# The second MLP's 36 token tiles as nodes of the list scheduler, with TensorE products costed shorter than they are

## The chip, the cores and the metric

The kernel runs on one core of a Trainium2 chip. The metric is the device time of one execution in microseconds (us). Before the change it is 1145.37 us, the median of three runs (1145.16 to 1147.82).

## What is computed

The inputs are float32, the two MLPs' weights float64. An attention with a packed middle step feeds a first MLP (512 to 2048 to 512, ELU), and that feeds the second MLP, which is what the change touches. The reference, cut to that part:

```python
x = _moe_ref(x=attention(q, k, v, p), ...)          # 4608 tokens x 512
def _moe2_ref(x, w_in, w_out, g_ln):
    h = x @ w_in                                     # 4608 x 1024
    e = np.exp(h - np.max(h, axis=-1, keepdims=True))
    solu = h * e / (np.sum(e, axis=-1, keepdims=True) + 1e-09)
    mu = np.mean(solu, axis=-1, keepdims=True)
    var = np.mean((solu - mu) ** 2, axis=-1, keepdims=True)
    ln = (solu - mu) / np.sqrt(var + 1e-06) * g_ln
    return (ln @ w_out).astype(np.float32)           # 4608 x 512
```

## The kernel before, in words

Every matmul operand is split into a rounded high part and a low remainder, and a product is three matmuls (`mm3`, L62 to L66). The split is a copy to the high part on ACT (L152) and a subtraction on DVE (L154).

**First part.** Attention and first MLP are written as nodes. A node (L591) has an engine, a planned duration, what it needs, which buffers it takes and frees, and a due time. `order()` (L889) is a list scheduler with a clock of its own: it works out for each node the latest start that still meets the due times (`late`), and then goes forward, always placing the node that can start first, and among those of one engine that can start within 0.3 us the one with the smallest `late`. Each engine runs its nodes in the order in which they were placed. This is fixed for PE, DVE, ACT and SP by `tc.manual_schedule` (L1015). The first MLP is 256 steps; a step is `ffn_h` (6 matmuls), two ACT passes (L433, L434), a DVE pass (L439), the split (L446, L449) and `ffn_x2` (12 matmuls). Its result is stored to DRAM (`x_dram`).

**Second MLP.** 4608 tokens are 36 tiles of 128. Nine loads (`load_x2`, L497) bring four tiles each, into the slots `wo0` to `wo2` or `wo3` to `wo5` in turn. Per tile i:

- `split_x2` (L504): one ACT cast and one DVE subtraction;
- `h2_mm` (L509): 24 matmuls of 128x512 into a two-bank PSUM tile: the single `misc` tile or one of two `acc` tiles, by i;
- `solu_ln` (L520): DVE max (nm, L523), ACT exp (L526), DVE sum and reciprocal (L527, L529), DVE product (z, L532), ACT square (L535, which frees the PSUM tile), DVE scale (L536), POOL power (L538), DVE normalisation (ln, L540);
- `t2_blocks` (L543): a transpose in 32x32 blocks on DVE (L547) and 16 block moves, 8 on DVE (L555) and 8 on ACT (L557);
- `t2_a` (L560): the split of the transposed tile into slot `wo6` or `wo7` (lnT, L152 and L154);
- `out_mm` (L566): 24 matmuls of 128x512 (the last tile's in two halves of 256 columns), the copy from PSUM (y, L578, ACT) and the store (L579, SP).

Only the first load, the splits of tiles 0 and 1 and the first product are nodes (L872 to L877). The rest follows in the program from L1024 on. For PE that order is kept (L1023): h2(0) among the last first-MLP steps, h2(1), h2(2), then h2(3), out(0), h2(4), out(1), ..., h2(35), out(32), out(33), out(34), out(35). For DVE, ACT and SP the framework orders these instructions itself with a timeline of its own, and can place them among the nodes of the first part:

```python
    for i in range(NTT):
        if i + 3 < NTT:
            h2_mm(i + 3)
        if i + 1 < NTT:
            t2_a(i + 1)
        if i + 2 < NTT:
            t2_blocks(i + 2)
        if i + 3 < NTT:
            solu_ln(i + 3)
```

Of the kernel before, what the change touches and what calls it, by code (L numbers as in the profile page):

```python
# [34 lines left out]
def attention_mlp_kernel(ctx: ExitStack, tc: tile.TileContext, q, k, v, v_tail, p,  # L35
# [461 lines left out]
    def load_x2(t):  # L497
        raw = slot(f"x2raw{t}", [P, 4, BLK], f"wo{3 * (t % 2)}", F32)
        sp.dma_start(out=raw, in_=x2_dram[:, :, t * BLK:(t + 1) * BLK])
        hi = slot(f"x2hi{t}", [P, 4, BLK], f"wo{3 * (t % 2) + 1}", F32R)  # L500
        lo = slot(f"x2lo{t}", [P, 4, BLK], f"wo{3 * (t % 2) + 2}", F32R)
        xs[t] = raw, hi, lo
# [14 lines left out]
                    kk == 0, kk == 3)  # L517
        last["h2", i] = o

    def solu_ln(i):  # L520
        o = last.pop(("h2", i)).rearrange("p a c -> p (a c)")
        nm = small.tile([P, 1], F32, tag="nm", name=f"nm2_{i}")
        dve.tensor_reduce(out=nm, in_=o, axis=AX.X, op=ALU.max, negate=True)  # L523
        e = work.tile([P, 5 * 4 * D], F32, tag="k", name=f"e3_{i}", bufs=1)[:, 0:DFF2]
        sm = small.tile([P, 1], F32, tag="sm", name=f"sm2_{i}")
        act.activation(e, o, AF.Exp, bias=nm, accum_out=sm)  # L526
        dve.tensor_scalar(out=sm, in0=sm, scalar1=1e-9, scalar2=None, op0=ALU.add)  # L527
        r = small.tile([P, 1], F32, tag="r", name=f"r2_{i}")
# [12 lines left out]
        last["ln", i] = ln

    def t2_blocks(i):  # L543


        t = big.tile([P, 4 * HS], F32, tag="AT", name=f"lnB{i}", bufs=3)[:, 0:DFF2]
        dve.transpose(t, last.pop(("ln", i)))  # L547
        o = big.tile([P, 4 * HS], F32, tag="AT", name=f"lnX{i}", bufs=3)[:, 0:DFF2]
        tv = t.rearrange("p (c a n) -> p c a n", a=4, n=NP)
        ov = o.rearrange("p (c n) -> p c n", n=P)  # L550
        for r in range(4):
            for a in range(4):
                x, y = ov[a * NP:(a + 1) * NP, :, r * NP:(r + 1) * NP], tv[r * NP:(r + 1) * NP, :, a]
                if (r + a) % 4 < 2:
                    dve.tensor_copy(x, y)  # L555
                else:
                    act.copy(x, y)  # L557
        last["t2", i] = o

    def t2_a(i):  # L560
        o = last.pop(("t2", i))
        t = slot(f"lnT{i}", [P, 2, 8, P], f"wo{6 + i % 2}", F32R)
        both(split(t[:, 0].rearrange("p c n -> p (c n)"), t[:, 1].rearrange("p c n -> p (c n)"), o))
        last["lnT", i] = t

    def out_mm(i):  # L566
        t = last.pop(("lnT", i))
        n = DM if i < NTT - 1 else DM // 2
        for c in range(0, DM, n):
            o = h_ps(f"o{i}_{c}")[:, 0:n]  # L570
            for x in range(2):
                for kk in range(8):
                    w, cs = wo2[kk // 2], slice((kk % 2) * DM + c, (kk % 2) * DM + c + n)
                    pe.matmul(o, t[:, x, kk], w[:, 0, cs], start=x + kk == 0, stop=x == 1 and kk == 7)  # L574
                    if x == 0:
                        pe.matmul(o, t[:, 0, kk], w[:, 1, cs], start=False, stop=False)  # L576
            y = work.tile([P, DM], F32, tag="at", name=f"y{i}_{c}", bufs=3)[:, 0:n]
            act.copy(y, o)  # L578
            sp.dma_start(out=out[i * P:(i + 1) * P, c:c + n], in_=y)  # L579
# [7 lines left out]
    def node(name, eng, us, needs, emit, takes=(), lets=(), due=None, size=0, behind=()):  # L591
# [277 lines left out]
    for i in range(2):  # L869
        pass  # L870
    end_due = FIRST_US + STEP_US * len(steps)
    node(("x2raw",), SP, 0.4, [("xout", 0, 1, 15, i) for i in range(2)] + [("xout", 0, 0, 15, i) for i in range(2)],  # L872
         lambda: load_x2(0), takes=[("wo0", "x2raw"), ("wo1", "x2hi"), ("wo2", "x2lo")], size=1.0)
    for i in range(2):
        split_nodes(("x2", i), lambda i=i: split_x2(i), needs=[("x2raw",)])
    node(("h2", 0), PE, 5.6, [("spD", "x2", 0)] + [("wi2", j) for j in range(4)],
         lambda: h2_mm(0), takes=[("misc", "h2")], due=end_due + 2)  # L877
# [11 lines left out]
    def order():  # L889
# [13 lines left out]
        def latest(name):  # L903

            stack = [name]
            while stack:
                x = stack[-1]
                wait = [y for y in then.get(x, ()) if y not in late]
                if wait:
                    stack += wait  # L910
                    continue
                stack.pop()
                v = nodes[x]
                ends = [late[y] for y in then.get(x, ())]
                if v["due"] is not None:
                    ends.append(v["due"])
                late[x] = min(ends, default=1e9) - v["us"] - (LATENCY[v["eng"]] + v["size"] * 2.9
                                                              if v["eng"] == SP else max(0.06, LATENCY[v["eng"]]))
            return late[name]
        for x in nodes:  # L920
# [94 lines left out]
    with tc.manual_schedule(engines={getattr(mybir.EngineType, e) for e in ("PE", "DVE", "Activation", "SP")}):  # L1015
        for x in order():
# [10 lines left out]
    solu_ln(1)  # L1027
    both(split_x2(3))
    t2_blocks(0)
    t2_a(0)  # L1030
    load_x2(1)
    h2_mm(2)
    t2_blocks(1)
    solu_ln(2)
    for i in range(NTT):
        if i + 3 < NTT:
            h2_mm(i + 3)
        if i + 1 < NTT:
# [45 lines left out]
```

## Time and profile before

| | |
|---|---|
| median of three runs | 1145.37 us |
| the profiled execution, own time | 1142.79 us |
| its span, first to last instruction | 1141.0 us |
| PE busy | 1114.4 us (98%) |
| DVE / ACT / POOL busy | 868.5 / 750.7 / 20.4 us |
| second MLP, first product to end | 731.5 to 1141.0 us |
| mean granted TensorE clock | 0.994 |

Times in the rows are microseconds from the span's start unless marked ns. "L574 PE" is an instruction of line 574 on TensorE; `lnT<-lnX` is output and input by the program's tile names; x8 is a count of merged instructions. In brackets stands how long the engine sat idle before the instruction and who ended that. A matmul's end is modelled, so starts are the safer reading on PE. In the trace the h2 products appear as `h<-wi,x2hi` and the out products as `o<-wo,lnT`.

### The profile page before, as it was taken

To read this page: it belongs to the slowest core of one execution; us is meant where nothing else is said; L and a number is where in the kernel's file an instruction comes from. 1 tells how busy PE (TensorE), PEld (TensorE's weight loads), DVE (VectorE), ACT (ScalarE), POOL (GpSimd) and SP (SyncE) were. 2 spreads that over 40 slices of the span, in tenths; PEclk is the share of its full clock that TensorE was granted. 3 is DMA by queue.
4 is the path that set the end of the run, shared out by engine and by line. 5 is a ranking of instruction groups with operands and counts; after the bars stand their busy time and mean duration, and the time that the engine had idled before them with its cause. 6 is when DMAs were issued, how large, how long until landed. Compare 5 with 4: busy or idle time off the path is not lost.

```text
span 1141.0 us, 21041 instructions
## 1 busy us (share of the span) xinstructions
PE 1114.4 (98%) x8164; PEld 984.1 (86%) x8164; DVE 868.5 (76%) x1956; ACT 750.7 (66%) x1627; POOL 20.4 (2%) x42
## 2 busy tenths in 40 slices
PE   8799999999999999999999999999999999999997
PEld 7588898899899899899899899878888888888886
DVE  5899897678777778777778644588877878878775
ACT  4688865666666765666665555567776776676674
POOL 0000000000000000000000000000000000000000
PEclk9899999999999999999999999999999999999999
DMA  9957334024133124233122322610202101000001
GB/s 344 342 174 260 105 104 125 24 82 139 59 121 121 59 103 139 77 103 121 59 101 99 111 95 65 215 52 34 65 19 65 56 28 65 19 28 20 28 28 38
DMA packets 56116, 111.07 MB, mean 97 GB/s; under 512 B 4432, under 2 KB 32336, under 8 KB 54224
## 3 DMA queue, kind: packets, MB, share of 16 engines
q1 hardware_dynamic: 56016, 109.73, 28.3%
q8 instruction: 64, 1.05, 0.4%
q14 instruction: 36, 0.29, 0.1%
HBM read 77.14 MB, written 32.57 MB: 96 GB/s over the span
## 4 chain that ended last, share of the span: by engine, by line
PE 54%; DVE 22%; ACT 15%; issue 6%; POOL 1%; DMA 1%; POOLq 0%; SPq 0%; ACTq 0%; DVEq 0%
PE acc L64 11%; PE acc L66 10%; PE acc L65 10%; ACT lnX L557 6%; PE h L64 6%; PE h L66 6%; PE h L65 6%; DVE lnB L547 4%; PE m L348 3%; DVE ln L540 2%; DVE z L532 2%; ACT h L535 2%; DVE lnT L154 2%; DVE nm L523 2%; PE s L348 2%
## 5 line engine op out<-in xcount | busy, mean ns | idle before, releaser
L64 PE MATMUL acc<-ghi,wo 128*128 128x288 f32 x1024 | 305.9, 299 | 0.6 <-DVE part L484 0.3
L66 PE MATMUL acc<-glo,wo 128*128 128x288 f32 x1024 | 301.6, 295 | 1.2 <-DVE glo L449 1.2
L65 PE MATMUL acc<-ghi,wo 128*128 128x288 f32 x1024 | 301.5, 294 | 0.0
L64 PEld LDWEIGHTS acc<-ghi,wo 128*128 128x128 f32 x1024 | 192.2, 188 | 22.0 <-ACT fe L433 9.1
L66 PEld LDWEIGHTS acc<-glo,wo 128*128 128x128 f32 x1024 | 192.4, 188 | 1.7 <-DVE glo L449 1.7
L65 PEld LDWEIGHTS acc<-ghi,wo 128*128 128x128 f32 x1024 | 192.3, 188 | 0.0
L574 PE MATMUL o<-wo,lnT 128*128 128x512 f32 (+1 forms) x592 | 185.0, 385 | 4.5 <-ACT lnT L152 4.5
L446 ACT CAST ghi<-fe 128x288 fp32r<-128x288 f32 x256 | 110.2, 431 | 103.5 <-DVE fe L439 102.7
L439 DVE SCALAR_TENSOR_TENSOR fe<-fe,h 128x288 f32<-128x288 f32 x256 | 115.3, 451 | 77.1 <-ACT fe L434 73.8
L557 ACT COPY lnX<-lnB 32x256 f32<-32x256 f32 x288 | 116.3, 404 | 78.1 <-DVE lnB L547 65.5
L64 PE MATMUL h<-AT,M 128*128 128x288 f32 x512 | 155.7, 304 | 10.6 <-DVE fe L439 9.0
L433 ACT ACTIVATE fe<-h 128x288 f32<-128x288 f32 x256 | 104.7, 409 | 91.3 <-PE h L66 85.9
L65 PE MATMUL h<-AT,M 128*128 128x288 f32 x512 | 151.6, 296 | 0.0
L66 PE MATMUL h<-AT,M 128*128 128x288 f32 x512 | 151.2, 295 | 0.3 <-DVE AT L154 0.3
L449 DVE TENSOR_TENSOR glo<-fe,ghi 128x288 fp32r<-128x288 f32 x256 | 115.3, 451 | 44.1 <-ACT ghi L446 41.8
L574 PEld LDWEIGHTS o<-wo,lnT 128*128 128x128 f32 x592 | 110.7, 189 | 27.4 <-ACT lnT L152 5.3
L64 PEld LDWEIGHTS h<-AT,M 128*128 128x128 f32 x512 | 96.3, 188 | 33.0 <-DVE fe L439 14.5
L434 ACT ACTIVATE fe<-fe 128x288 f32<-128x288 f32 x256 | 113.9, 445 | 8.0
L576 PE MATMUL o<-wo,lnT 128*128 128x512 f32 (+1 forms) x296 | 113.8, 386 | 0.0
L64 PE MATMUL h<-wi,x2hi 128*128 128x512 f32 x288 | 112.3, 390 | 1.3 <-ACT h L535 1.3
L66 PE MATMUL h<-wi,x2hi 128*128 128x512 f32 x288 | 112.1, 389 | 0.0
L65 PE MATMUL h<-wi,x2lo 128*128 128x512 f32 x288 | 112.1, 389 | 0.0
(101 smaller groups left out, 1613.5 us busy)
## 6 DMA issues: line engine op xcount, KB each, us to landing
k<-in_k SPq DMA_DIRECT2D x32, 288.0 KB, 3.5
q<-in_q SPq DMA_DIRECT2D x16, 576.0 KB, 4.5
x_dram<-x SPq DMA_DIRECT2D x32, 288.0 KB, 2.8
x2raw<-x_dram SPq DMA_DIRECT2D x9, 1024.0 KB, 5.6
out_x<-y SPq DMA_DIRECT2D x35, 256.0 KB, 2.0
raw_wi<-in_w_in SPq DMA_DIRECT2D x8, 1024.0 KB, 9.6
v<-in_v SPq DMA_DIRECT2D x16, 512.0 KB, 5.2
w_dram<-w SPq DMA_DIRECT2D x16, 512.0 KB, 2.9
```

The costliest lines, as they stand in the source:

```text
L64: pe.matmul(o, a[0], b[0], start=start, stop=False)
L65: pe.matmul(o, a[1], b[0], start=False, stop=False)
L66: pe.matmul(o, a[0], b[1], start=False, stop=stop)
L348: pe.matmul(o[u * NP:(u + 1) * NP, r], w[rows, u, :], x[rows, u, :], start=True, stop=True)
L433: act.activation(e, o[:, 0:HS], AF.Relu, scale=-1.0)
L434: act.activation(e, e, AF.Exp, scale=-1.0)
L439: dve.scalar_tensor_tensor(out=e, in0=e, scalar=-1.0, in1=o[:, 0:HS], op0=ALU.add, op1=ALU.max)
L446: act.copy(ghi, e)
L449: dve.tensor_tensor(out=glo, in0=e, in1=ghi.bitcast(F32), op=ALU.subtract)
L557: act.copy(x, y)
L574: pe.matmul(o, t[:, x, kk], w[:, 0, cs], start=x + kk == 0, stop=x == 1 and kk == 7)
L576: pe.matmul(o, t[:, 0, kk], w[:, 1, cs], start=False, stop=False)
```

## The change

`solu_ln` is cut into eight pieces (max, exp, reciprocal, z, square, variance, power, normalisation), `t2_blocks` into the transpose and 16 moves, `out_mm` into product, copy and store. The instructions are the same but for one thing: of the last tile's 16 moves DVE takes 12 and ACT 4. All pieces of all 36 tiles become nodes, with buffers and due times, and POOL becomes an engine of the scheduler. The hand-written order at the end is gone. Each h2 or out product is costed 4.6 us.

```diff
+    end_due = FIRST_US + STEP_US * len(steps) + 2
+    H2_US = 4.6
+    for t in range(NTT * P // BLK):
+        xs_of = [(tag, (f"x2{what}", t)) for tag, what in zip((f"wo{3 * (t % 2) + n}" for n in range(3)), ("raw", "hi", "lo"))]
...
+        node(("x2raw", t), SP, 0.4, [("xout", n // 2, n % 2, NF - 1, i) for n in halves for i in range(2)],
+             lambda t=t: load_x2(t), takes=xs_of, size=1.0)
...
+        out_due = end_due + (4 + 2 * i) * H2_US
+        h2_due = end_due + i * H2_US if i < 4 else out_due - 7 * H2_US
+        bank = ("misc" if i % 3 == 0 or i == 1 else "acc", ("h2", i))
...
+        node(("h2", i), PE, H2_US, [("spD", "x2", i)] + ([("wi2", j) for j in range(4)] if i == 0 else []),
+             lambda i=i: h2_mm(i), takes=[bank], due=h2_due,
...
+        node(("so_max", i), DVE, 1.22, [("h2", i)], lambda i=i: so_max(i))
+        node(("so_exp", i), ACT, 1.33, [("so_max", i)], lambda i=i: so_exp(i), takes=[e3])
+        node(("so_rec", i), DVE, 0.33, [("so_exp", i)], lambda i=i: so_rec(i))
+        node(("so_z", i), DVE, 1.5, [("so_rec", i)], lambda i=i: so_z(i), takes=[z], lets=[e3])
+        node(("so_sqr", i), ACT, 1.33, [("so_z", i)], lambda i=i: so_sqr(i), lets=[bank])
+        node(("so_var", i), DVE, 0.16, [("so_sqr", i)], lambda i=i: so_var(i))
+        node(("so_pow", i), POOL, 0.55, [("so_var", i)], lambda i=i: so_pow(i))
...
+        node(("so_ln", i), DVE, 0.82, [("so_pow", i)], lambda i=i: so_ln(i), takes=[ln], lets=[z], due=end + 8.3)
+        node(("t2", i), DVE, 1.25, [("so_ln", i)], lambda i=i: t2_blocks(i), takes=[lnb], lets=[ln], due=end + 10.5)
...
+                eng = DVE if (r + a) % 4 < 2 or i == NTT - 1 and (r + a) % 4 < 3 else ACT
+                moves.append(node(("t2m", i, r, a), eng, 0.29 if eng == DVE else 0.4,
...
+        split_nodes(("lnT", i), lambda i=i: t2_split(i), needs=moves, takes=[lnt], lets=[lnx], us=(1.06, 1.24))
...
+            node(("out", i, c), PE, H2_US * n / DM, [("spD", "lnT", i)] + ([("wo2", j) for j in range(4)] if i == 0 else []),
+                 lambda i=i, c=c, n=n: out_mm(i, c, n), takes=[o], lets=[lnt], due=out_due + (c > 0) * 2.7)
+            node(("yc", i, c), ACT, 0.58, [("out", i, c)], lambda i=i, c=c, n=n: y_copy(i, c, n), takes=[y], lets=[o],
+                 due=out_due + 8)
+            node(("ys", i, c), SP, 0.4, [("yc", i, c)], lambda i=i, c=c, n=n: y_store(i, c, n), lets=[y], size=0.25)
...
-    ctx.enter_context(tc.manual_schedule(engines={mybir.EngineType.PE}))
-    solu_ln(0)
-    both(split_x2(2))
-    h2_mm(1)
...
-        out_mm(i)
```

## Rows read from the trace of the kernel before

**Rows 1.** The page's first part: busy time of the engines.

```profile
PE 1114.4 (98%) x8164; PEld 984.1 (86%) x8164; DVE 868.5 (76%) x1956; ACT 750.7 (66%) x1627; POOL 20.4 (2%) x42
```

**Rows 2.** Windows by stage: length, busy per engine, then clock, DMA share, GB/s.

```profile
715.00:731.00 16.00, 14.37 (x106) 13.91 (x105) 8.20 (x17) 10.19 (x23) 0.00 (x0) 1.00 0.78 274
731.00:760.00 29.00, 27.73 (x141) 23.45 (x140) 20.25 (x43) 14.64 (x30) 1.11 (x2) 1.00 0.17 57
760.00:1119.80 359.80, 359.80 (x1589) 297.85 (x1587) 293.24 (x625) 250.00 (x493) 18.09 (x33) 1.00 0.11 39
1119.80:1138.00 18.20, 13.56 (x73) 11.36 (x72) 8.76 (x19) 9.68 (x20) 0.55 (x1) 0.91 0.14 52
1138.00:1141.00 3.00, 0.00 (x0) 0.00 (x0) 0.00 (x0) 0.24 (x1) 0.00 (x0) 0.92 0.13 44
```

**Rows 3.** Timeline: out(1) and out(32) begin, and the max of tiles 4 and 35.

```profile
771.67 0.39 PE L574 MATMUL o<-wo,lnT 128*128 128x512 f32 x1
...
774.12 1.21 DVE L523 TENSOR_REDUCE nm<-h 128x1 f32<-128x1024 f32 x1
...
1108.95 0.39 PE L574 MATMUL o<-wo,lnT 128*128 128x512 f32 x1
...
1116.46 1.19 DVE L523 TENSOR_REDUCE nm<-h 128x1 f32<-128x1024 f32 x1
```

**Rows 4.** Waits, 760 to 1119.8 us: total us, times, longest.

```profile
ACT lnX L557 <- DVE lnB L547: 60.4, 24, 3.4
...
DVE sm L527 <- ACT e L526: 19.6, 16, 1.2
DVE ln L540 <- POOL rs L538: 19.2, 26, 1.1
...
DVE lnT L154 <- ACT lnT L152: 8.3, 9, 1.2
```

**Rows 5.** Timeline of the tail: the last products, and the last tile's chain.

```profile
1122.59 0.50 PE L574 MATMUL o<-wo,lnT 128*128 128x512 f32 x1 [2.60 <-ACT lnT L152]
...
1125.02 0.63 PE L576 MATMUL o<-wo,lnT 128*128 128x512 f32 x1
...
1131.83 0.39 PE L574 MATMUL o<-wo,lnT 128*128 128x256 f32 x1 [1.88 <-ACT lnT L152]
...
1127.39 2.37 DVE L555 COPY lnX<-lnB 32x256 f32<-32x256 f32 x8
1131.81 1.22 DVE L154 TENSOR_TENSOR lnT<-lnX,lnT 128x1024 fp32r<-128x1024 f32 x1 [2.04 <-ACT lnT L152]
...
1127.39 3.31 ACT L557 COPY lnX<-lnB 32x256 f32<-32x256 f32 x8 [2.57 <-DVE lnB L547]
1130.73 1.04 ACT L152 CAST lnT<-lnX 128x1024 fp32r<-128x1024 f32 x1
1131.68 0.58 ACT L578 COPY y<-o 128x512 f32<-128x512 f32 x1
```

**Rows 6.** Timeline: tile 0's chain, from its max to its last subtraction.

```profile
737.02 0.29 PE L64 MATMUL h<-AT,M 128*128 128x288 f32 x1
...
737.22 1.23 DVE L523 TENSOR_REDUCE nm<-h 128x1 f32<-128x1024 f32 x1 [2.29 <-PE h L66]
...
750.88 1.23 DVE L154 TENSOR_TENSOR lnT<-lnX,lnT 128x1024 fp32r<-128x1024 f32 x1 [0.35 <-ACT lnT L152]
```

**Rows 7.** Timeline, end of the first MLP: the casts of x2 tiles, and PE.

```profile
720.09 1.14 ACT L152 CAST x2hi<-x2raw 128x512 fp32r<-128x512 f32 x2 [1.24 <-DMA x2raw<-x_dram]
...
723.60 2.17 ACT L152 CAST x2hi<-x2raw 128x512 fp32r<-128x512 f32 x4
...
726.65 0.40 PE L64 MATMUL h<-AT,M 128*128 128x288 f32 x1 [1.55 <-DVE fe L439]
```

**Rows 8.** Timeline, PE: the first matmuls of h2(1) and h2(3).

```profile
743.52 0.50 PE L64 MATMUL h<-wi,x2hi 128*128 128x512 f32 x1 [0.77 <-ACT h L535]
...
755.22 0.50 PE L64 MATMUL h<-wi,x2hi 128*128 128x512 f32 x1 [0.51 <-ACT h L535]
```

**Rows 9.** Waits of the SP queue from 760 us, and the page's x2 loads (last: us to landing).

```profile
SPq L579 <- ACT y L578: 283.4, 28, 14.7
...
x2raw<-x_dram SPq DMA_DIRECT2D x9, 1024.0 KB, 5.6
```

More of the change, by code (lines that the diff above doesn't have):

```diff
@@ L527, in solu_ln, with so_rec @@
+    def so_rec(i):
+        sm = last.pop(("sm", i))
+        r = last["r", i] = small.tile([P, 1], F32, tag="r", name=f"r2_{i}")
         dve.tensor_scalar(out=sm, in0=sm, scalar1=1e-9, scalar2=None, op0=ALU.add)
-        r = small.tile([P, 1], F32, tag="r", name=f"r2_{i}")
         dve.reciprocal(r, sm)
-        z = work.tile([P, 5 * 4 * D], F32, tag="q", name=f"z{i}", bufs=1)[:, 0:DFF2]
-        su = small.tile([P, 1], F32, tag="su", name=f"su{i}")
-        dve.scalar_tensor_tensor(out=z, in0=o, scalar=r, in1=e, op0=ALU.mult, op1=ALU.mult, accum_out=su)
@@ L540, in solu_ln, with so_z @@
-        dve.tensor_scalar(out=ln, in0=z, scalar1=su, scalar2=rs, op0=ALU.add, op1=ALU.mult)
-        last["ln", i] = ln
+    def so_z(i):
+        z = last["z", i] = work.tile([P, 5 * 4 * D], F32, tag="q", name=f"z{i}", bufs=1)[:, 0:DFF2]
+        su = last["su", i] = small.tile([P, 1], F32, tag="su", name=f"su{i}")
+        dve.scalar_tensor_tensor(out=z, in0=last["o", i], scalar=last.pop(("r", i)), in1=last.pop(("e", i)),
+                                 op0=ALU.mult, op1=ALU.mult, accum_out=su)
+        dve.tensor_scalar(out=su, in0=su, scalar1=-1.0 / DFF2, scalar2=None, op0=ALU.mult)
@@ new lines, in so_sqr, with so_var, so_pow @@
+    def so_sqr(i):
+        sq = last["sq", i] = small.tile([P, 1], F32, tag="sq", name=f"sq{i}")
+        act.activation(last.pop(("o", i)), last["z", i], AF.Square, bias=last["su", i], accum_out=sq)
+    def so_var(i):
+        sq = last["sq", i]
+        dve.tensor_scalar(out=sq, in0=sq, scalar1=1.0 / DFF2, scalar2=1e-6, op0=ALU.mult, op1=ALU.add)
+    def so_pow(i):
+        rs = last["rs", i] = small.tile([P, 1], F32, tag="rs", name=f"rs{i}")
+        nc.gpsimd.tensor_tensor(out=rs, in0=last.pop(("sq", i)), in1=mhalf, op=ALU.pow)
@@ L543, in t2_blocks, with so_ln @@
+    def so_ln(i):
+        ln = last["ln", i] = work.tile([P, DFF2], F32, tag="stage", name=f"ln{i}", bufs=2)
+        dve.tensor_scalar(out=ln, in0=last.pop(("z", i)), scalar1=last.pop(("su", i)), scalar2=last.pop(("rs", i)),
+                          op0=ALU.add, op1=ALU.mult)
     def t2_blocks(i):
-        t = big.tile([P, 4 * HS], F32, tag="AT", name=f"lnB{i}", bufs=3)[:, 0:DFF2]
+        t = last["lnB", i] = big.tile([P, 4 * HS], F32, tag="AT", name=f"lnB{i}", bufs=3)[:, 0:DFF2]
         dve.transpose(t, last.pop(("ln", i)))
-        o = big.tile([P, 4 * HS], F32, tag="AT", name=f"lnX{i}", bufs=3)[:, 0:DFF2]
@@ L549, in t2_blocks @@
[L549 to L579, printed above, removed]
@@ L585, in attention_mlp_kernel, with t2_move @@
-    ENGINES = PE, DVE, ACT, SP = "PE", "DVE", "ACT", "SP"
+    def t2_move(i, r, a, eng):
+        if ("lnX", i) not in last:
+            last["lnX", i] = big.tile([P, 4 * HS], F32, tag="AT", name=f"lnX{i}", bufs=3)[:, 0:DFF2]
+        tv = last["lnB", i].rearrange("p (c a n) -> p c a n", a=4, n=NP)
+        ov = last["lnX", i].rearrange("p (c n) -> p c n", n=P)
+        x, y = ov[a * NP:(a + 1) * NP, :, r * NP:(r + 1) * NP], tv[r * NP:(r + 1) * NP, :, a]
+        if eng is act:
+            act.copy(x, y)
+        else:
+            dve.tensor_copy(x, y)
@@ new lines, in t2_split, with out_mm @@
+    def t2_split(i):
+        t = last["lnT", i] = slot(f"lnT{i}", [P, 2, 8, P], f"wo{6 + i % 2}", F32R)
+        return split(t[:, 0].rearrange("p c n -> p (c n)"), t[:, 1].rearrange("p c n -> p (c n)"), last.pop(("lnX", i)))
+    def out_mm(i, c, n):
+        t = last["lnT", i]
+        o = last["y", i, c] = h_ps(f"o{i}_{c}")[:, 0:n]
+        for x in range(2):
+            for kk in range(8):
+                w, cs = wo2[kk // 2], slice((kk % 2) * DM + c, (kk % 2) * DM + c + n)
+                pe.matmul(o, t[:, x, kk], w[:, 0, cs], start=x + kk == 0, stop=x == 1 and kk == 7)
+                if x == 0:
+                    pe.matmul(o, t[:, 0, kk], w[:, 1, cs], start=False, stop=False)
@@ L586, in attention_mlp_kernel, with y_copy, y_store @@
+    def y_copy(i, c, n):
+        y = work.tile([P, DM], F32, tag="at", name=f"y{i}_{c}", bufs=3)[:, 0:n]
+        act.copy(y, last.pop(("y", i, c)))
+        last["y", i, c] = y
+    def y_store(i, c, n):
+        sp.dma_start(out=out[i * P:(i + 1) * P, c:c + n], in_=last.pop(("y", i, c)))
+    ENGINES = PE, DVE, ACT, SP, POOL = "PE", "DVE", "ACT", "SP", "POOL"
     CAPS = dict(misc=1, acc=2, h=2, fe=2, ghi=4, glo=4, at=3, AT=3, cv=2, stage=2, xo=2)
-    LATENCY = {PE: 0.2, DVE: -0.02, ACT: -0.03, SP: 1.9}
+    LATENCY = {PE: 0.2, DVE: -0.02, ACT: -0.03, SP: 1.9, POOL: 0.1}
@@ L868, in attention_mlp_kernel @@
         step_nodes(n)
[L869 to L877, printed above, removed]
+    end_due = FIRST_US + STEP_US * len(steps) + 2
@@ new lines, in attention_mlp_kernel @@
+    H2_US = 4.6
+    for t in range(NTT * P // BLK):
+        xs_of = [(tag, (f"x2{what}", t)) for tag, what in zip((f"wo{3 * (t % 2) + n}" for n in range(3)), ("raw", "hi", "lo"))]
+        halves = range(t * BLK // HS, (t * BLK + BLK - 1) // HS + 1)
+        node(("x2raw", t), SP, 0.4, [("xout", n // 2, n % 2, NF - 1, i) for n in halves for i in range(2)],
+             lambda t=t: load_x2(t), takes=xs_of, size=1.0)
+    ends = defaultdict(list)
+    for i in range(NTT):
+        t = i * P // BLK
+        out_due = end_due + (4 + 2 * i) * H2_US
+        h2_due = end_due + i * H2_US if i < 4 else out_due - 7 * H2_US
+        bank = ("misc" if i % 3 == 0 or i == 1 else "acc", ("h2", i))
+        e3, z, ln, lnb, lnx = ("k", ("e3", i)), ("q", ("z", i)), ("stage", ("ln", i)), ("AT", ("lnB", i)), ("AT", ("lnX", i))
+        split_nodes(("x2", i), lambda i=i: split_x2(i), needs=[("x2raw", t)], lets=[(f"wo{3 * (t % 2)}", ("x2raw", t))])
+        node(("h2", i), PE, H2_US, [("spD", "x2", i)] + ([("wi2", j) for j in range(4)] if i == 0 else []),
+             lambda i=i: h2_mm(i), takes=[bank], due=h2_due,
+             lets=[(f"wo{3 * (t % 2) + n}", (f"x2{what}", t)) for n, what in ((1, "hi"), (2, "lo"))])
+        node(("so_max", i), DVE, 1.22, [("h2", i)], lambda i=i: so_max(i))
[5 more added lines that the diff above has]
+        node(("so_pow", i), POOL, 0.55, [("so_var", i)], lambda i=i: so_pow(i))
+        end = h2_due + H2_US
+        node(("so_ln", i), DVE, 0.82, [("so_pow", i)], lambda i=i: so_ln(i), takes=[ln], lets=[z], due=end + 8.3)
+        node(("t2", i), DVE, 1.25, [("so_ln", i)], lambda i=i: t2_blocks(i), takes=[lnb], lets=[ln], due=end + 10.5)
+        moves = []
+        for r in range(4):
+            for a in range(4):
+                eng = DVE if (r + a) % 4 < 2 or i == NTT - 1 and (r + a) % 4 < 3 else ACT
+                moves.append(node(("t2m", i, r, a), eng, 0.29 if eng == DVE else 0.4,
+                                  [("t2", i), moves[0] if moves else None],
+                                  lambda i=i, r=r, a=a, eng=eng: t2_move(i, r, a, dve if eng == DVE else act),
+                                  takes=[] if moves else [lnx], lets=[lnb], due=end + 11 + len(moves) / 2))
+        lnt = (f"wo{6 + i % 2}", ("lnT", i))
+        split_nodes(("lnT", i), lambda i=i: t2_split(i), needs=moves, takes=[lnt], lets=[lnx], us=(1.06, 1.24))
+        n = DM if i < NTT - 1 else DM // 2
+        for c in range(0, DM, n):
+            o, y = ("h", ("o", i, c)), ("at", ("y", i, c))
+            node(("out", i, c), PE, H2_US * n / DM, [("spD", "lnT", i)] + ([("wo2", j) for j in range(4)] if i == 0 else []),
[3 more added lines that the diff above has]
+            node(("ys", i, c), SP, 0.4, [("yc", i, c)], lambda i=i, c=c, n=n: y_store(i, c, n), lets=[y], size=0.25)
@@ L916, in latest @@
                     ends.append(v["due"])
[L917 removed]
+                late[x] = min(ends, default=1e4) - v["us"] - (LATENCY[v["eng"]] + v["size"] * 2.9
                                                               if v["eng"] == SP else max(0.06, LATENCY[v["eng"]]))
```

39 lines of the change are left out of this document (7 added, 32 removed).

## The prediction

> **What bounds the kernel now.** I read the busy times first: PE is busy for 98% of the span, no other engine above 76% [rows 1]. The windows by stage then show where the missing 2% lies for the stage the change touches [rows 2]: from 760 to 1119.8 us PE is busy for 359.80 of 359.80 us, while DVE has work for 293.24 and ACT for 250.00. PE's idle time stands at the edges: 1.63 us (16.00 - 14.37) just before the stage, 1.27 us (29.00 - 27.73) at its head, 4.64 us (18.20 - 13.56) in the tail, and 3.0 us of last copy and store behind the last product.
>
> PE's pace comes from two starts: out(1) begins at 771.67 and out(32) at 1108.95 [rows 3], 31 tiles in 337.28 us, so 10.88 us a tile and 5.44 us a product. That is no wait on anybody. What the change can win is therefore in the edges; in the middle it can only keep the pace or lose it.
>
> **The tail, where the profile has most to give.** h2(4) has just ended when out(1) begins, and its max starts at 774.12, 2.4 us later; h2(35) ends as out(32) begins, at 1108.95, and its max starts at 1116.46, 7.5 us later [rows 3]. So DVE and ACT, run tile by tile with waits on each other, fall 5.1 us further behind over 31 tiles. Until the tail a stock of ready tiles hides that. The waits say where it comes from [rows 4]: ACT stands 60.4 us for the block transpose, DVE 19.6 us for the exp, 19.2 us for POOL's power, 8.3 us for the cast. Behind h2(35) PE has only three products left. Dense, out(34) would start at 1108.95 + 2 x 5.44 = 1119.83 and out(35) at 1125.27. They start at 1122.59 and 1131.83 [rows 5], each waiting for its lnT. The end is 1131.83 - 1125.27 = **6.56 us** late. [...]
>
> **The change, part by part.**
>
> *Same instructions.* Nothing is added but a new split of the last tile's moves. The middle costs and gains nothing on PE as long as DVE's and ACT's load fits: 359.8 / 10.88 = 33.1 tiles, so DVE 293.24 / 33.1 = 8.87 and ACT 250.00 / 33.1 = 7.56 us a tile against 10.88. DVE has 2.0 us a tile left for waits, ACT 3.3. The PE order by the new due times is the old one: h2(i) is due seven products before out(i), which lies behind h2(i+3).
>
> *Tail.* If one tile's waits are filled with another tile's work, the lag of 7.5 us goes. The chain alone is bounded by tile 0, which ran with little beside it: max at 737.22, lnT ready at 750.88 + 1.23 = 752.11, hence 14.9 us, and 0.2 us from the product's end (737.02) to the max [rows 6]. For tile 35: 1108.95 + 0.2 + 14.9 = 1124.05. With DVE's 12 moves at 2.37 / 8 = 0.296 us (3.56) in place of ACT's 8 in 3.31 us [rows 5] add 0.25: 1124.3. PE wants it at 1125.27, so 1.0 us to spare. Against that stands what is left of tile 34: at most its DVE moves and subtraction, 2.37 + 1.22 = 3.6 us, and two y copies of 0.58 us on ACT [rows 5]. All of it in the way makes 3.6 + 1.2 - 1.0 = 3.8 us late, none of it 0. DVE is without work of its own in this chain during exp, square, power and cast, so about half should fit: I take 1.4 us late and 6.56 - 1.4 = **5.2 us won** (2.8 to 6.6). Late next would be the last subtraction of tile 35, as now, only less.
>
> [...]
>
> *End of the first MLP.* There the framework had put casts of later x2 tiles into ACT's queue: two that wait 1.24 us for the load, then four in a row of 2.17 us, and PE waits 1.55 us for the step behind them [rows 7]; the window loses 1.63 in all. As nodes with late due times they fall into gaps one at a time. But the first still waits for its load, whose landing the plan only estimates. I take **1.0 us won** (-1.2, one more wait of 1.24 us, to 1.6).
>
> *Head.* h2(1) waits 0.77 us and h2(3) 0.51 us for the square that frees `misc` [rows 8]. From the max to that square's end takes 743.52 - 737.22 = 6.3 us, more than a product of 5.44, so waiting stays where PE has nothing else. For h2(1) it has nothing (the `acc` tiles are still the first MLP's). In place of h2(3) the scheduler can take h2(4), whose bank is free. I take **0.5 us won** (-0.8, one more such wait, to 1.3).
>
> *Queues.* SP's nine loads and 37 stores change places. SP now stands at the stores for most of the stage (283.4 us, in 28 waits [rows 9]), so a load can stand behind a store that waits for its copy: a tile, 10.9 us. The load takes 5.6 us. The plan issues load t+2 once h2(4t+3) frees its slots, four tiles (43.5 us) before h2(4t+8) begins. Cover 43.5 against 16.5: nothing. If that cover went, PE would wait at every fourth tile. The y copy stands in ACT's queue behind its product; who waits behind it is the second rival.
>
> *Sum.* 5.2 + 1.0 + 0.5 = 6.7 us. The profiled execution took 1142.79 us (span 1141.0), 2.6 below the median of 1145.37. I subtract from the median: 1145.4 - 6.7 = **1138.7 us**. The bounds together: 0.8 to 9.5 us, or 1144.6 to 1135.9.
>
> **The rivals.**
>
> *A: the tail's wait only changes its name.* The interleaved order leaves work of tiles 33 and 34 in front of tile 35, as the price of keeping everybody busy. For: DVE has 8.87 of 10.88 us filled, so a tile's chain in company takes longer than 14.9 us. Against: the due times put older tiles first, and 16.3 us of products cover the chain. With all 3.8 us of collisions and no gain at head and first MLP, 2.8 us: 1142.6, or no change I can tell (a measurement tells about 0.3%, 3.4 us). That the order comes out much as it was, lag and all, gives 1145 and belongs here. Chance 0.15.
>
> *B: slower, ACT's queue stands at the y copies.* The plan's products take 4.6 us, the chip's 5.44: the plan ends a product 0.84 us early, puts its copy into ACT's queue there, and the chip holds up every move and cast queued behind it, then DVE behind those, tile after tile. It decides from the point where a tile's waits pass DVE's 2.0 us of room: each further 0.3 us is 34 x 0.3 = 10.2 us, of which the stock hides about the 5.1 us that it hides now. At 0.6 us over: 20.4 - 5.1 = 15.3, less head and first MLP (1.5): 1145.4 + 13.8 = 1159. For: two copies' worth of error a tile, 1.7 us, is near that room. Against: the plan shortens the others too. A move costs it 0.29 less 0.08 us where the chip takes 0.296 [rows 5], so plan and chip stretch by like factors; and with six products between h2(i) and out(i), a late copy alone makes no lnT late. Chance 0.13.
>
> [...] The trace agrees: where ACT stood 1.24 us for a load, the first MLP's step that PE wanted stayed queued behind the casts [rows 7].
>
> **How the numbers follow.** Forecast 0.72, A 0.15, B 0.13. Time of the likeliest: 1138.7. The range goes from 1135.5 (all 9.5 us won, and 0.4 for the spread of runs) to 1145.5, which takes in A and leaves out B and a little. Faster by over 3.4 us: the forecast but for its low edge, and nothing of A, 0.72. Within: 0.15. Slower: 0.13.
>
> **What would show it.** Right: the max of tile 35 starts within 2 us of h2(35)'s end; out(34) without a wait and out(35) with under 2 us; the window's clock near 1.00; no run of four casts before 727 us; DVE no longer waiting for the power 26 times; PE at 10.88 us a tile. Wrong: idle time on PE between tiles 5 and 32, ending on lnT or on a square, with ACT's y copy waiting for PE in most tiles (B), or out(34) and out(35) still waiting 4 us together (A).

## The result and the profile after

The changed kernel takes 1135.66 us (median of 5 runs, 1134.98 to 1137.68) against 1145.37 us before (median of 5 runs of the same chip). The ratio is 0.9916, with a 95% interval of 0.9902 to 0.9931: 9.7 us less, where 6.7 were forecast. The profiled execution of after took 1136.66 us, its span is 1134.9 us.

The page and the windows by stage answer to [rows 1, 2]. The first line is from the page of after (busy time of the engines):

```profile
PE 1114.6 (98%) x8164; PEld 986.6 (87%) x8164; DVE 875.0 (77%) x1960; ACT 752.0 (66%) x1623; POOL 25.9 (2%) x42
```

The windows of after come next: length, busy per engine in the order PE, PEld, DVE, ACT, POOL, then clock, DMA share, GB/s. The first three are stages as in [rows 2], the last three run between the same events in both kernels:

```profile
715.00:731.00 16.00, 16.00 (x123) 16.00 (x122) 8.58 (x18) 10.44 (x24) 0.00 (x0) 1.00 0.74 254
731.00:760.00 29.00, 28.05 (x147) 24.18 (x146) 19.92 (x40) 15.48 (x30) 1.10 (x2) 1.00 0.19 63
760.00:1119.80 359.80, 359.80 (x1589) 298.00 (x1588) 304.51 (x639) 258.18 (x501) 24.14 (x34) 1.00 0.12 42
...
721.70:743.58 21.88, 21.88 (x149) 20.90 (x148) 13.35 (x26) 12.94 (x29) 0.00 (x0) 1.00 0.30 101
743.58:772.22 28.64, 27.69 (x124) 22.70 (x123) 22.91 (x47) 16.28 (x31) 1.65 (x3) 1.00 0.18 58
...
1109.50:1125.82 16.32, 16.32 (x74) 13.52 (x73) 13.50 (x32) 10.45 (x20) 0.55 (x1) 1.00 0.09 32
```

The same three stretches in the kernel before:

```profile
718.44:742.46 24.02, 22.39 (x149) 20.95 (x148) 13.17 (x26) 12.59 (x29) 0.00 (x0) 1.00 0.51 180
742.46:771.67 29.21, 27.94 (x123) 22.62 (x122) 24.51 (x50) 19.51 (x39) 1.66 (x3) 1.00 0.19 66
...
1108.95:1131.83 22.88, 18.41 (x74) 14.39 (x72) 16.00 (x37) 15.87 (x32) 1.09 (x2) 0.93 0.10 35
```

PE's work is the same (8164 matmuls, 98%), and what went is idle time at the edges. The three stretches run from the ACT pass of the 251st of the first MLP's 256 steps to the last matmul of that MLP (149 matmuls in both), from there to out(1), and from out(32) to out(35) (74 in both). Measured like this the kernels can be compared although the profiled execution of after came to that ACT pass 3.3 us later (721.70 against 718.44). That delay is not the change's: up to 700 us the two traces hold the same instructions in the same order on PE, DVE, ACT and POOL, 3.4 us are lost by the sixth step already, and the same kernel once more reached the 251st step 0.8 us behind the kernel before.

- end of the first MLP: 24.02 - 21.88 = 2.14 us won. All 1.63 us of idle time (24.02 - 22.39) are gone, and PE is busy 0.51 us less for the same matmuls;
- head: 29.21 - 28.64 = 0.57 us won;
- middle: out(1) to out(32) takes 1109.50 - 772.22 = 337.28 us, to the hundredth what it took before [rows 3];
- tail: 22.88 - 16.32 = 6.56 us;
- behind out(35): 1141.0 - 1131.83 = 9.17 before, 1134.9 - 1125.82 = 9.08 after, 0.1 us.

That makes 9.4 us, which agrees with the 9.7 us of the medians. The spans alone differ by 6.1 us, because of the 3.3 us at the start. So each experiment below is given by its median and by "the aligned time", which runs from the first h matmul of the 251st step to the end of the span: 423.54 us before, 414.18 after.

What the waits became, in the same stretch as [rows 4] (after, 760 to 1119.8 us: total us, times, longest):

```profile
ACT e L528 <- DVE nm L523: 76.7, 29, 3.5
DVE nm L523 <- PE h L66: 24.2, 22, 4.0
DVE ln L557 <- POOL rs L553: 15.7, 27, 0.7
...
ACT lnX L573 <- DVE lnB L564: 3.4, 4, 0.9
```

ACT's 60.4 us for the block transpose are 3.4, and DVE's 19.6 us for the exp are no longer on the list. DVE and ACT now wait for the max and for h2, that is for PE: they have caught up with it. DVE still waits for the power 27 times (26 before).

The tail of after, by start (timeline of PE, DVE and ACT; it answers to [rows 3, 5]):

```profile
1109.50 0.39 PE L587 MATMUL o<-wo,lnT 128*128 128x512 f32 x1
1109.70 1.23 DVE L523 TENSOR_REDUCE nm<-h 128x1 f32<-128x1024 f32 x1 [1.22 <-PE h L66]
...
1110.95 1.12 ACT L528 ACTIVATE e<-h,nm 128x1024 f32<-128x1024 f32 x1 [3.50 <-DVE nm L523]
1112.18 2.90 ACT L573 COPY lnX<-lnB 32x256 f32<-32x256 f32 x7
1115.11 1.12 ACT L545 ACTIVATE h<-z,su 128x1024 f32<-128x1024 f32 x1
...
1119.46 0.88 DVE L575 COPY lnX<-lnB 32x256 f32<-32x256 f32 x3
1120.37 1.22 DVE L154 TENSOR_TENSOR lnT<-lnX,lnT 128x1024 fp32r<-128x1024 f32 x1
...
1121.63 2.68 DVE L575 COPY lnX<-lnB 32x256 f32<-32x256 f32 x9
1124.39 1.05 ACT L152 CAST lnT<-lnX 128x1024 fp32r<-128x1024 f32 x1 [1.56 <-DVE lnX L575]
1125.13 0.96 PE L587 MATMUL o<-wo,lnT 128*128 128x512 f32 x4
1125.47 1.22 DVE L154 TENSOR_TENSOR lnT<-lnX,lnT 128x1024 fp32r<-128x1024 f32 x1 [1.17 <-ACT lnT L152]
```

h2(35) ends as out(32) begins, at 1109.50; its max starts 0.2 us later (7.5 before). ACT's seven moves of tile 34 lie between the exp and the square of tile 35; in tile 0 of the kernel before ACT stood idle there for 1.92 us. The cast ends at 1124.39 + 1.05 = 1125.44, and out(35), whose first matmul starts at 1125.82 (it is the last of the four that the row of 1125.13 merges with the end of out(34)), never waits. The granted clock is 1.00 from out(32) to out(35), where it was 0.93 before.

### The profile page after: what moved, and what is told of

Same layout as the page of the kernel before. It is cut to its first block, busy times and chain, and to the rows that moved or that the text cites. A ratio compares the mean times of both kernels' runs of the same rounds, so it can differ in the third digit from the quotient of the medians.

```text
span 1134.9 us, 20973 instructions
## 1 busy us (share of the span) xinstructions
PE 1114.6 (98%) x8164; PEld 986.6 (87%) x8164; DVE 875.0 (77%) x1960; ACT 752.0 (66%) x1623; POOL 25.9 (2%) x42
## 3 DMA queue, kind: packets, MB, share of 16 engines
q8 instruction: 64, 1.05, 0.4%
## 4 chain that ended last, share of the span: by engine, by line
PE 90%; DVE 5%; ACT 4%; issue 1%; DVEq 0%; ACTq 0%
PE h L64 12%; PE o L587 12%; PE acc L64 11%; PE h L65 11%; PE h L66 11%; PE acc L66 10%; PE acc L65 10%; PE o L589 6%; PE m L348 3%; PE s L348 2%; PE spare L1076 1%; PE pp L328 1%; DVE fe L439 1%; PE pp L317 1%; DVE glo L449 1%
```

## The experiments

The theory, from here T: the interleaving of the tile chains is the cause, filling each tile's waits with other tiles' work. The rivals: C, the short product cost of 4.6 us does it (later split in two: P, the plan's slack itself is needed; C2, it only makes up for DVE and ACT steps that the plan costs too low); M, the last tile's 12 to 4 split of moves does it; F, it is enough that the hand-written order of every engine is kept as written. "Lag" is the time from h2(35)'s end to its max: 7.5 us before, 0.2 after. e1 to e4 shared a chip, with a median of 1145.08 us for the kernel before.

**e1: the product at its real cost.**

```diff
-    H2_US = 4.6
+    H2_US = 5.45
```

> The changed kernel with each product costed 5.45 us, what it takes, in place of 4.6. Theory O (order: the gain is DVE's and ACT's interleaved order, and the product's cost only the plan's clock): within 1.5 us of the changed kernel's 1135.7, PE busy for all of 760 to 1119 us, out(34) and out(35) without a wait. Rival C (the short cost itself makes DVE and ACT run ahead): the lag of the max behind h2 comes back in part, PE waits 2 us or more in the tail, 1139 or more.

Measured: 1143.75 us, ratio 0.9984 (0.9973 to 0.9994); lag 8.96 us, more than before. Up to the end of the last h2 it takes 388.80 us from the 251st step, exactly as after (391.50 before): the whole loss lies in the tail. The timeline of ACT and PE: tile 34's exp and square, its moves, the next exp, and the start of out(34):

```profile
1105.36 1.12 ACT L528 ACTIVATE e<-h,nm 128x1024 f32<-128x1024 f32 x1 [0.29 <-DVE nm L523]
1108.56 1.12 ACT L545 ACTIVATE h<-z,su 128x1024 f32<-128x1024 f32 x1 [1.99 <-DVE su L541]
...
1112.85 3.31 ACT L573 COPY lnX<-lnB 32x256 f32<-32x256 f32 x8 [1.62 <-DVE lnB L564]
1116.51 1.12 ACT L528 ACTIVATE e<-h,nm 128x1024 f32<-128x1024 f32 x1 [0.35 <-DVE nm L523]
...
1122.41 0.80 PE L587 MATMUL o<-wo,lnT 128*128 128x512 f32 x1 [4.94 <-ACT lnT L152]
```

ACT does all eight moves of a tile before the next exp (in 22 of the 32 tiles from tile 4 on; in after in none), so nothing is left to fill the time from exp to square. Here it is 1116.51 - 1105.36 = 11.15 us from exp to exp where PE needs 10.88: this tile falls 0.27 us further behind. From tile 4 to tile 35 the lag grows from 0.8 to 8.96 us, 0.26 us a tile. In the waits (760 to 1119 us):

```profile
ACT h L545 <- DVE su L541: 52.9, 30, 2.4
ACT lnX L573 <- DVE lnB L564: 43.3, 25, 2.8
...
DVE sq L549 <- ACT h L545: 22.5, 22, 1.4
```

The same nodes with another cost give back most of the gain. T alone, that making nodes of the steps is enough, falls; C holds as to the outcome.

**e2: the last tile's moves 8 and 8.**

```diff
-                eng = DVE if (r + a) % 4 < 2 or i == NTT - 1 and (r + a) % 4 < 3 else ACT
+                eng = DVE if (r + a) % 4 < 2 else ACT
```

> The changed kernel with the last tile's moves 8 on DVE and 8 on ACT, as for every other tile. Theory O: ACT's four moves of the last tile begin at 1121.19, behind the y copy of out(33); with eight of 0.414 us they end at 1124.5 instead of 1122.8, and the cast starts about 0.1 us later than its 1124.39. 0.4 us were to spare: no change, 1135.7 within 1.5. Rival M (the 12 to 4 split wins the tail): out(35) waits 2 us or more, 1138 or more.

Measured: 1135.13 us, ratio 0.9909 (0.9892 to 0.9926), aligned 414.09. The timeline of ACT in its tail:

```profile
1121.42 3.32 ACT L573 COPY lnX<-lnB 32x256 f32<-32x256 f32 x8
1124.77 1.05 ACT L152 CAST lnT<-lnX 128x1024 fp32r<-128x1024 f32 x1
```

Tile 35's max starts at 1109.93 here, so its cast ends 1124.77 + 1.05 - 1109.93 = 15.89 us behind it, 0.15 us later than in after (15.74). The room covers that, and out(35) follows without a wait. M falls.

**e3: the kernel before, with the framework's freedom taken from its hand-written part.**

```diff
-    ctx.enter_context(tc.manual_schedule(engines={mybir.EngineType.PE}))
+    ctx.enter_context(tc.manual_schedule(engines={getattr(mybir.EngineType, e) for e in ("PE", "DVE", "Activation", "SP")}))
```

> The kernel before with DVE, ACT and SP also held to the order that is written by hand for the second MLP, no plan. Rival F (the gain is that the framework no longer reorders these engines): 1136 to 1140. Theory O: the hand order runs each tile's chain in one piece; DVE's 8.87 us a tile plus waits for exp 1.4, square 1.4 and power 0.75 is 12.4 us against PE's 10.88, 33 tiles of 1.5 us less some 10 us of stock: slower than before, 1160 to 1195.

Measured: 1252.37 us, ratio 1.0933 (1.0902 to 1.0963), slower than any theory had it. The waits (760 to 1230 us) say what the sum had missed:

```profile
ACT lnX L557 <- DVE lnB L547: 92.8, 34, 3.1
...
PE h L64 <- ACT x2hi L152: 44.8, 32, 16.3
```

The split of the next x2 tile is written behind the whole chain of a tile, and h2 waits for it at every tile (32 times). So the order as written is worse than what the framework had made of it, and F falls: the kernel before already had some interleaving, of casts and splits, from the framework.

**e4: the kernel before, with only the first eight x2 splits and their second load as planned nodes.**

```diff
-    for i in range(2):
-        split_nodes(("x2", i), lambda i=i: split_x2(i), needs=[("x2raw",)])
+    node(("x2raw1",), SP, 0.4, [("xout", 0, 1, 15, i) for i in range(2)] + [("xout", 1, h, 15, i) for h in range(2) for i in range(2)],
+         lambda: load_x2(1), takes=[("wo3", "x2raw1"), ("wo4", "x2hi1"), ("wo5", "x2lo1")], size=1.0)
+    for i in range(8):
+        split_nodes(("x2", i), lambda i=i: split_x2(i), needs=[("x2raw",) if i < 4 else ("x2raw1",)])
...
-    both(split_x2(2))
-    both(split_x2(3))
-    load_x2(1)
...
-            if i + 4 < NTT:
+            if 8 <= i + 4 < NTT:
```

> The kernel before with one part of the change: the loads of the first two x2 blocks and the splits of tiles 0 to 7 as nodes of the plan; all the rest as before. Theory O: PE's idle time of 1.6 us between 715 and 731 us goes and nothing else: 1143.4 to 1143.8. If that idle time had another cause: 1145.4, and the window still short of 16 us.

Measured: 1143.51 us, ratio 0.9983 (0.9971 to 0.9995). The first window of [rows 2] in e4, and the tail:

```profile
715.00:731.00 16.00, 16.00 (x120) 15.91 (x120) 8.47 (x18) 10.66 (x26) 0.00 (x0) 1.00 0.79 277
...
1119.80:1138.00 18.20, 14.66 (x72) 12.86 (x72) 8.63 (x18) 8.42 (x18) 0.55 (x1) 0.81 0.14 52
```

PE has no idle time left in the first one, and up to the last h2 the kernel is 391.50 - 389.35 = 2.15 us shorter than before: the planned casts alone give the 2.14 us of after's first stage. The tail is that of the kernel before (lag 7.54). The aligned time is 422.91, against 423.54, so 2.15 - 0.63 = 1.5 us went back in this profiled execution's tail, where the clock was 0.81 (0.91 in [rows 2]); from 1129 to 1138 us it was 0.81, in the kernel before 1.00. From 1133.0 to 1134.9 us it was 0.50, and out(35)'s matmuls started 0.21 us apart there, where at 1.00 the kernel before took 0.12. out(34) and out(35) waited as long as before (2.63 and 1.90 us).

**e5: a product costed still shorter.** e5 to e8 shared another chip, with a median of 1145.68 us for the kernel before; beside the last three kernels it took 1145.2.

```diff
-    H2_US = 4.6
+    H2_US = 3.6
```

> The changed kernel with products costed 3.6 us. Theory P (packing: a product costed short leaves the plan no slack, so it fills DVE's waits for exp and square with the moves of the tile before): the order stays packed, 1135.7 within 1.5, PE dense from 760 to 1119 us. Rival B (the y copy now stands in ACT's queue ahead of the cast and the moves and holds them up until the real product ends): lag of the max and waits of PE on lnT in the tail, 1140 or more.

Measured: 1138.14 us, ratio 0.9933 (0.9916 to 0.9949), aligned 417.16; lag 0.32. Its waits from 760 to 1140 us, and one of its y copies in the timeline of ACT:

```profile
ACT y L593 <- PE o L587: 63.2, 32, 3.4
...
DVE lnT L154 <- ACT lnT L152: 35.9, 27, 1.4
```

```profile
1103.52 0.59 ACT L593 COPY y<-o 128x512 f32<-128x512 f32 x1 [1.93 <-PE o L587]
1104.00 1.05 ACT L152 CAST lnT<-lnX 128x1024 fp32r<-128x1024 f32 x1
```

This is rival B's mechanism at work: the plan ends a product 1.8 us early, the copy stands at the head of ACT's queue 1.93 us for it, and the cast and the moves behind it are late, then DVE's subtraction. It costs 417.16 - 414.18 = 3.0 us, all of it in the tail, where out(34) waits 1.22 us and out(35) 0.64 us for the cast. B's 13.8 us are far off, as PE stayed dense to 1119 us. In these rows ACT kept to the order of its queue: the tile's last move, one of DVE's, ended at 1102.42, ACT stood idle, and the cast started only when the copy ended, at 1103.52 + 0.59 = 1104.11 but for 0.1 us of overlap.

**e6: h2(0) due 6 us earlier.**

```diff
-        h2_due = end_due + i * H2_US if i < 4 else out_due - 7 * H2_US
+        h2_due = end_due + i * H2_US - 6 * (i == 0) if i < 4 else out_due - 7 * H2_US
```

> The changed kernel with h2(0) due 6 us earlier, so that it runs two steps before the end of the first MLP. Theory O: the chain to the square that frees the PSUM tile (6.3 us) is covered by the remaining first-MLP products, h2(1)'s wait of 1.0 us goes, PE is busy for 29.0 of the 29 us from 731 to 760, 1134.7. Rival: the last first-MLP step, now later, opens an equal gap: 1135.7.

Measured: 1134.59 us, ratio 0.9901 (0.9884 to 0.9919). The head's window:

```profile
731.00:760.00 29.00, 29.00 (x157) 25.33 (x156) 20.76 (x42) 15.73 (x31) 1.11 (x2) 1.00 0.18 58
```

The head's last wait (0.95 us in after, at h2(1)) is gone, and the aligned time is 413.36, 0.8 us less. The intervals of the two ratios overlap, so this shows in the trace only.

**e7: in the changed kernel, each exp behind ACT's moves of the tile before.**

```diff
-        node(("so_exp", i), ACT, 1.33, [("so_max", i)], lambda i=i: so_exp(i), takes=[e3])
+        node(("so_exp", i), ACT, 1.33, [("so_max", i)] + [("t2m", i - 1, r, a) for r in range(4) for a in range(4) if i and (r + a) % 4 > 1], lambda i=i: so_exp(i), takes=[e3])
```

> The changed kernel with one order forced: a tile's exp needs all eight ACT moves of the tile before, so these can no longer fill the time between exp and square. Theory P: DVE waits again for exp, square and power, the max falls behind h2 by several us by tile 35, out(34) and out(35) wait 3 us or more together, 1139 or more. Rival O2 (the tail is won by the due times, not by what fills the waits): 1135.7 within 1.5.

Measured: 1174.35 us, ratio 1.0247 (1.0226 to 1.0267), aligned 453.15. Two exps of its timeline, and its waits from 760 to 1119 us:

```profile
1102.25 1.12 ACT L528 ACTIVATE e<-h,nm 128x1024 f32<-128x1024 f32 x1
...
1113.88 1.12 ACT L528 ACTIVATE e<-h,nm 128x1024 f32<-128x1024 f32 x1
```

```profile
ACT lnX L573 <- DVE lnB L564: 106.9, 29, 7.7
DVE sm L533 <- ACT e L528: 49.6, 29, 2.2
...
PE o L587 <- ACT lnT L152: 12.9, 25, 0.8
```

One order put back on one engine brings back the waits of [rows 4], larger, and a loop of 1113.88 - 1102.25 = 11.63 us a tile. PE's stock of ready tiles runs out and it waits for the cast 25 times; out(34) and out(35) wait 5.5 us together. The max of tile 35 starts only 2.6 us behind its h2, not the several us expected, because PE itself now runs at the slower loop. That is what T says of the moves between exp and square.

**e8: all costs true**, the product 5.45, and five DVE and ACT steps that the plan had too short (reciprocal, z, normalisation, transpose, moves) raised to what the chip takes once the plan has taken off its 0.08 us.

```diff
-    H2_US = 4.6
+    H2_US = 5.45
...
+        node(("so_rec", i), DVE, 0.45, [("so_exp", i)], lambda i=i: so_rec(i))
+        node(("so_z", i), DVE, 1.59, [("so_rec", i)], lambda i=i: so_z(i), takes=[z], lets=[e3])
...
+        node(("so_ln", i), DVE, 0.92, [("so_pow", i)], lambda i=i: so_ln(i), takes=[ln], lets=[z], due=end + 8.3)
+        node(("t2", i), DVE, 1.36, [("so_ln", i)], lambda i=i: t2_blocks(i), takes=[lnb], lets=[ln], due=end + 10.5)
...
+                moves.append(node(("t2m", i, r, a), eng, 0.38 if eng == DVE else 0.495,
```

> The changed kernel with products at 5.45 us and the second MLP's DVE and ACT steps at what they take (a DVE move 0.30, an ACT move 0.415, z 1.51, normalisation 0.84, transpose 1.28, each plus the 0.08 that the scheduler takes off). Rival C2 (the short product only makes up for DVE and ACT costed too low): no lag, 1135.7 within 1.5. Theory P (it is the plan's slack that leaves waits unfilled): the square's wait is filled only in part, a lag remains and the tail waits, 1139 or more.

Measured: 1135.92 us, ratio 0.9911 (0.9895 to 0.9926), aligned 414.22, lag 0.2: the changed kernel again, without a short product. P falls, C2 holds.

**e9: the product 5.45 and only the moves' costs true.**

```diff
-    H2_US = 4.6
+    H2_US = 5.45
...
-                moves.append(node(("t2m", i, r, a), eng, 0.29 if eng == DVE else 0.4,
+                moves.append(node(("t2m", i, r, a), eng, 0.38 if eng == DVE else 0.495,
```

> As the run with all true costs, but of the DVE and ACT steps only the 16 moves are costed at what they take (0.38 and 0.495 with the 0.08 that is taken off); products at 5.45 us. Theory V (the moves' missing 0.08 to 0.1 us each is what the short product made up for): no lag, 1135.7 within 1.5. Rival W (the small steps around z, normalisation and transpose count too, 0.3 us a tile): part of the lag comes back, 1138 to 1142.

Measured: 1135.39 us, ratio 0.9913 (0.9899 to 0.9927), aligned 414.23, lag 0.2. It differs from e1 in one line. The waits that answer to e1's (760 to 1119 us):

```profile
ACT lnX L573 <- DVE lnB L564: 48.6, 25, 2.8
ACT h L545 <- DVE su L541: 34.4, 29, 2.0
...
DVE sq L549 <- ACT h L545: 14.3, 18, 1.4
```

So it is the moves. The plan takes 0.08 us off each DVE and ACT step when it frees the engine, and so counts a DVE move 0.21 us and an ACT move 0.32; the chip takes 2.37 / 8 = 0.296 and 3.31 / 8 = 0.414 [rows 5]. That is 8 x 0.09 = 0.7 us a tile on each engine. With a true product the plan then believes that ACT finishes a tile's moves before the next exp (e1), and nothing is left for the gap. The product cut by 0.85 us puts moves into the gap by another route: with these plans one of the two had to change, the moves' cost or the product's. Which of the two engines' moves matters was not run.

The traces let this be counted. Of the 32 tiles from tile 4 on, ACT has no move between exp and square in 23 in the kernel before, 22 in e1 and 32 in e7, the three that fall behind; in 10 in e9, and in none in e8 and after. What goes with the lag is DVE's idle time, not ACT's. ACT's wait for the transpose, the largest of [rows 4], is 48.6 us in e9 and 49.2 in e8, which end without a lag, and 43.3 in e1, which has the longest. DVE's waits for ACT and POOL together (760 to 1119 us) are 59.1 us in the kernel before, 70.3 in e7 and 45.4 in e1, but 34.6 in e9, 27.0 in e8 and 17.5 in after.

**e10: e8 with e6's due time.** To e8's edit is added

```diff
-        h2_due = end_due + i * H2_US if i < 4 else out_due - 7 * H2_US
+        h2_due = end_due + i * H2_US - 6 * (i == 0) if i < 4 else out_due - 7 * H2_US
```

> All true costs and h2(0) due 6 us earlier, the two together. Theory O: they act at different places, so the head's wait goes as it did alone: 1134.9 (1135.9 less 1.0), PE dense from 715 us to the last product. Rival: with the true costs the order at the head is another and a wait comes back: 1136.

Measured: 1133.87 us, ratio 0.9898 (0.9884 to 0.9912), aligned 413.41: the lowest median of the study.

**The changed kernel once more**, unedited, beside e9 and e10.

> The changed kernel once more, beside the two above on one chip: 1135.7 within 1.0, 0.7 to 1.2 above the run with h2(0) early.

Measured: 1134.52 us, ratio 0.9906 (0.9892 to 0.992), aligned 414.19, within 0.01 us of the first profile. That is 0.2 us below the band expected, and 0.65 above e10, where 0.7 to 1.2 were expected. Its interval overlaps those of e6 and e10, so that these two beat it by 0.8 us is a reading of the traces, not of the times.

## Why the prediction was right, and where its sizes were off

The direction and the mechanism held: the gain came from the edges, the middle kept its pace to the hundredth, the time lies in the range and below the point forecast by 3.0 us. That it lies in the range is partly luck: 1135.66 is 0.16 us above the low edge, the 9.7 us won are more than the 9.5 of all bounds together, and the same kernel once more took 1134.52, outside it, beside a kernel before at 1145.2.

**The tail: the step that failed is the chain counted to the last subtraction.** The prediction took 14.9 us from tile 35's max to lnT ready, 1.0 us to spare, 2.4 us of collisions, 1.4 us late, 5.2 us won. The row it had in hand says otherwise: out(35) waited in the kernel before for "ACT lnT L152", the cast [rows 5]. The product's first matmuls use the high part alone; the subtraction was in both kernels still running when out(35) began (after: 1125.47 to 1126.69, the product at 1125.82). Counted to the cast, the chain of tile 0 is 749.80 + 1.05 - 737.22 = 13.63 us [rows 6], by this row of ACT's timeline before:

```profile
749.80 1.05 ACT L152 CAST lnT<-lnX 128x1024 fp32r<-128x1024 f32 x1
```

In tile 35 of after, from 1109.70 to 1125.44, it is 15.74, 2.1 us more: 0.25 for the 12 moves, as forecast, 1.25 for tile 34's subtraction between DVE's moves, at 1120.37, and the rest, 0.6, mostly for ACT's moves of tile 34 ahead of the square (which starts 5.41 us after the max, in tile 0 5.01). So the collisions were 1.85 rather than 2.4 us, and the room was 1125.27 - (1108.95 + 0.2 + 13.63 + 0.25) = 2.2 rather than 1.0. Nothing was late: 6.56 us won, the upper end of the term.

**Where the lag came from.** The prediction spread it evenly, 5.1 us over 31 tiles, and put ACT's wait for the transpose first. The trace of the kernel before has it in steps: from exp to exp a tile takes 10.82 us where no x2 split falls in, just under PE's 10.88, but each group of four tiles with its four splits takes 44.2 us where PE needs 43.5; behind the last splits, which end at 1034.6 us, the lag levels off (7.9 us at tile 29, 7.5 at tile 35). So with its waits DVE had no room left for the splits. Whether splits planned for all tiles, with the rest of the kernel before as it is, would have won the tail too was not run; e4 planned the first eight alone and kept the lag of 7.54.

**End of the first MLP: 1.0 forecast, 2.1 measured.** The first four casts went one at a time between the steps' own ACT work (four more in a row came at 735.39, and PE did not wait for what stood behind them); the wait for the load is half as long (0.61 us for 1.24) and PE does not feel it. The timeline of ACT in after, to be read beside [rows 7]:

```profile
723.20 0.62 ACT L152 CAST x2hi<-x2raw 128x512 fp32r<-128x512 f32 x1 [0.61 <-DMA x2raw<-x_dram]
723.72 0.43 ACT L446 CAST ghi<-fe 128x288 fp32r<-128x288 f32 x1
724.06 0.61 ACT L152 CAST x2hi<-x2raw 128x512 fp32r<-128x512 f32 x1
```

The bound of 1.6 counted idle time only. The same 149 matmuls were also busy for 0.51 us longer before: a matmul's end is modelled, so a second, shorter halt there, at 722.46 (0.37 us from start to start where the pace is 0.13), counts as busy but for 0.08 us, and the first matmul after each halt took 0.40 us where most take 0.29 [rows 7, 6]. e4 gets the same 2.15 us from this part alone.

**Head: 0.5 forecast, 0.57 measured.** PE took h2(4) ahead of h2(3) in after, as forecast, and the wait of h2(3) is gone; h2(1) still waits for the square, 0.95 us in place of 0.77. e6 shows that this wait was in reach too, by a due time.

**Middle and queues: nothing, right.** 337.28 us in both. SP waits for the y copies longer than before (367.3 us for 308.8 from 760 us on), and no h2 waited for a load.

**The sum** was 6.7, by stages it is 9.4: of the 2.7 more, 1.4 come from the tail, 1.1 from the first MLP, and 0.2 from the head and the end.

**What would show it.** The clock, the lag, the run of casts and the pace came as written. One sign failed: DVE still waits for the power 27 times, 15.7 us in place of 19.2. The tail was won without filling this wait.

**The rivals.** A did not come about, but e1 comes out as A describes, lag and all, from one number in the plan; its due times put older tiles first too, so that was no argument against. B's mechanism exists (e5) and costs 3 us at twice the error. The argument against B, that plan and chip stretch by like factors, holds in direction only: the chip takes 5.44 / 4.6 = 1.18 times the plan's product, but 0.296 / 0.21 = 1.41 times its DVE move and 0.414 / 0.32 = 1.29 times its ACT move. e1, e8 and e9 show what follows: with the plan's moves 0.09 us too cheap, a true product is the one that is out of proportion. The prediction did not see that correcting the product alone would lose what the change wins.

## What to carry to other kernels

In a planned order the proportions of the costs can count more than the costs themselves: find the cheap operation that occurs sixteen times a tile and compare its cost in the plan with its pitch on the chip, before you bend the cost of the big one. When a chain decides, count it to the operand that the first waiting instruction reads, which the profile names, not to the end of the group that makes it. Compare two profiles between the same events inside the kernel where a part that varies lies ahead of them.

## What the runs showed of the hardware

POOL's power, one column, takes 0.55 or 0.56 us in all 36 tiles before. In after 13 of 36 are clearly longer. The timeline of POOL and DVE for the longest, and the last tile's:

```profile
796.45 1.63 POOL L553 TENSOR_TENSOR rs<-sq,mhalf 128x1 f32<-128x1 f32 x1 [9.26 <-DVE sq L549]
796.45 1.22 DVE L154 TENSOR_TENSOR lnT<-lnX,lnT 128x1024 fp32r<-128x1024 f32 x1
...
1116.68 0.55 POOL L553 TENSOR_TENSOR rs<-sq,mhalf 128x1 f32<-128x1 f32 x1 [10.33 <-DVE sq L549]
```

The power that starts together with a subtraction of two SBUF inputs takes 1.08 us longer, not much under the 1.22 that the subtraction lasts; one that starts 0.23 us into such a subtraction takes 1.40. Eleven others start 0.23 us into an x2 subtraction of 0.68 and take 0.86, which is 0.31 longer, where 0.45 of the subtraction was left. All 13 end 0.41 us behind the end of the subtraction, which is itself no longer than elsewhere, so each is longer by what was left of it less 0.14 us; one power that met only the last 0.10 us of a subtraction took 0.55. Four more take 0.58, beside one of DVE's block moves. Beside the max, which reads PSUM, the power took 0.55 (seven times before). The trace shows the delays, not what makes them. They cost PE nothing here: out(1) to out(32) takes 337.28 us as before, and the last tile's power met no subtraction and took 0.55 us.
